# Drawing twelve steps of the next batch's transform into each round, and spacing steps wider from round 4 on

## The chip, the core and the metric

The kernel runs on one core of a Trainium2 chip. The metric is the device time of one execution in microseconds (us). Before the change the median of three runs is 1286.0 us (1285.17 to 1287.41).

## What is computed

A Fourier mixing layer is followed by a mixture of experts in which every token goes to one expert.

```python
X = np.fft.fft(np.fft.fft(x, axis=1), axis=2).real      # x: (8, 2496, 256)
x = X.reshape(19968, 256)
logits = x @ w_gate                                     # 8 experts
e = argmax(logits, axis=1)
gate = softmax(logits)[n, e]
out[n] = gate * (relu(x[n] @ w1[e]) @ w2[e])            # w1: 256x1024, w2: 1024x256
```

## The kernel before

**Transform.** Each of the 8 batches is transformed in two stages. `first(b)` (L327) loads the batch in three pieces `xq` (L291, 0.9 MB each), folds them on DVE (L297 to L299, L308), multiplies them on PE (product `s`, `half1` at L313), copies the product to `t` on ACT (L323) and writes it to DRAM as `Td` (L344, 448 KB each). It has twelve yields, so twelve steps, three for each q from 0 to 3: those of q = 0 only fold, those of q = 3 only multiply. In the third step of q = 1, 2 and 3 it writes a `Td` piece and asks for one piece of the batch after (`load`, L346). `ahead_of(b)` (L888) runs `first(b)` and then `regroup` (L353), which reads `Td` back in another order into `t4` with two DMAs of 768 and 640 KB, in packets of 1 KB.

`second(b)` (L363) works on `t4`: `turn_last` (product `pr`), `group` (product `p<-table,t`, evicted by ACT into `zz`), then ten steps in two halves of five, each with a product `p<-table,zz` that gives a tile of transformed rows and their logits. After each half `route` (L418) finds the expert and the place of each row, in four parts; the third is the PE product `rk`. At its end ten row tiles are put in `waiting`. `send` (L464) takes one from there, converts its places on ACT (L469) and scatters it to `Xs` with an indirect DMA that POOL issues (L237). `close(b)` runs `plan` (L478), which works out on DVE which expert each block of the round has; its tables then stand in `tabs`. `through(b)` waits until all row tiles of the batch have been sent, and then puts the batch in `whole`.

`mixed(b)` (L894) weaves these into the steps of one round: three steps of `ahead_of(b + 1)`; then `second(b)` with 19 yields, after every other one of which a step of `ahead_of(b + 1)` is run; then `close(b)` with the `regroup` of batch b + 1; then `through(b)`.

**Experts.** `experts` (L713) runs blocks of 512, 256 or 128 sorted tokens, one expert to a block. A block fetches its rows `xb` from `Xs` and 2 MB of weights `w_sb`, both on SP's queue and up to three blocks ahead. Its first product is `ph` (or, in blocks of 512 tokens from batch 3 on, seven products with the tiles `a` to `e`), evicted as `hT` by ACT and DVE in turn (L810, L808); its second product is `py` from `hT`, evicted by ACT as `y` (L849) and scattered to the output. `hT` has one buffer. Batch 0 gives two blocks of 256 and four of 128, batch 1 four of 256, batch 2 three of 512, batches 3 to 6 five of 512 each, batch 7 five of 512 and the rest.

**The order around the change.** The whole order is written out by hand: each engine's instructions stand in the order in which this code issues them. The loop at L954 has one turn for each round b from 1 to 7. In it the blocks of batch b - 1 run, with the steps of `mixed(b)` beside them. Each yield of `experts` brings a weight w and says whether it is "full" (no step may follow it) or open. For an open one, `due` grows by

```python
due += TICKS * w / ((SHARE if b >= LATE else EARLY) * open_) if w else 1
```

(L971), and one step is run for each whole 1 in `due`. `open_` is the open weight of the round: 32 in rounds 1 and 2, 48 in round 3, 40 in rounds 4 to 7. `TICKS` is 32, so a round's first 32 steps take 70% of its open weight in rounds 1 to 3 and 60% in rounds 4 to 7. In round 1 the steps of batch 0's `close` and `through`, and what is left of `early` (batch 1), are woven with those of `mixed(1)` (L958). Steps left over when the blocks are done are run in a row (L981).

Of the kernel before, what the change touches and what calls it, by code (L numbers as in the profile page):

```python
# [3 lines left out]

# [1 line left out]

# [14 lines left out]
B, S, D = 8, 2496, 256  # L21
# [110 lines left out]
def rounds():  # L132

    want = [((256, 2), (128, 4)), ((256, 4),)] + [((512, B),)] * (B - 2)
    plan, used = [], 0

    def full(done, size):
        return max(0, -(-(done - used - E * (size - 1)) // size))  # L140

    for b in range(B):
        done = (b + 1) * S
        now = []
        for size, most in want[b]:
            k = min(full(done, size), most)
            if k:
                now.append((size, k, False))
            used += size * k
        if b == B - 1:  # L150
            k = full(done, BLK)
            used += BLK * k
            now.append((BLK, k, False))
            now.append((REST, (NT - used + E * (REST - 1)) // REST, True))
        plan.append(now)
    return plan
# [27 lines left out]

TICKS = 32
LATE = 4
SHARE, EARLY, ROOM = 0.6, 0.7, 1.2
WARM = 16
MOST = max(k for now in rounds() for _, k, _ in now)

# [1 line left out]
def halved(b, size):  # L192

    return size == 512 and b > 2 or size == 256 and b == B - 1
# [22 lines left out]
def kernel(ctx: ExitStack, tc, x, w_gate, w1, w2, out):  # L217
# [49 lines left out]
    side = [n for n in consts if n not in ("w1", "rt")]  # L267
# [196 lines left out]
    def send():  # L464

        if waiting:
            b, place, idx, rows = waiting.popleft()
            if b:
                act.copy(idx, place)  # L469
            sent(put_row(Xs, idx, rows, E * CAP - 1, "xs"), b)  # L470
# [397 lines left out]
    def woven(*parts):  # L868
        parts = list(parts)
        while parts:  # L870
            for p in list(parts):
                if next(p, p) is p:
                    parts.remove(p)
                else:
                    yield

    def close(b):

        for size, k, last in rounds()[b]:
            yield from plan(b, size, k, last)  # L880

    def through(b):

        while waiting and waiting[0][0] == b:
            yield
        whole.add(b)

    def ahead_of(b):  # L888

        yield from first(b)  # L890
        regroup(b, 0)
        regroup(b, 1)

    def mixed(b):  # L894

        one, two = (ahead_of(b + 1) if b + 1 < B else iter(())), second(b)
        for _ in range(3):
            next(one, None)
            yield
        for k, _ in enumerate(two):  # L900
            if k % 2:
                next(one, None)
            yield
        yield from woven(close(b), one)
        yield from through(b)
# [43 lines left out]
    for k, _ in enumerate(second(0)):  # L949
        if k % 2 == 0:  # L950
            next(early, None)
        send()
    work = experts(todo)
    for b in range(1, B):  # L954

        side, done, due, room = mixed(b), 0, 0.0, 0.0
        if b == 1:
            side = woven(chain(close(0), through(0)), chain(early, side))  # L958
        blocks = [(size, k * size / BIG, halved(b - 1, size)) for size, k, _ in rounds()[b - 1]]
        total = sum(k * (15 if seven_ else 16) for _, k, seven_ in blocks)  # L960
        open_ = sum(k * (8 if seven_ else 16) for _, k, seven_ in blocks)
        while done < total:
            w, full = next(work)
            done += w
            if full and not w:

                while waiting:
                    send()
                whole.update(p[0] for p in tabs if p != "cnt")
            if not full:  # L970
                due += TICKS * w / ((SHARE if b >= LATE else EARLY) * open_) if w else 1  # L971
            while due >= 1:
                next(side, None)
                due -= 1
                if b < LATE or not w:
                    send()
            room = min(room + (w if full else 0.75 * w), 2)
            if b >= LATE and room >= ROOM:
                send()
                room -= ROOM  # L980
        for _ in side:  # L981
            send()
# [52 lines left out]
```

## Time and profile before

| view | value |
|---|---|
| profiled execution | 1297.33 us (span 1295.5 us) |
| median of the runs | 1286.0 us |
| mean granted TensorE clock | 0.971 |
| DVE, ACT, POOL busy | 700.5, 423.4, 360.6 us |
| DMA over the span | 249.75 MB, 193 GB/s |
| PE's longest waits by line: `s` on DVE's fold | 10.9 us in 3 |
| `pt` on the rows `xb` | 7.3 us in 2 |
| `ph` on `hT` by DVE | 6.7 us in 3 |

The profiled execution is 11.3 us longer than the median, so a stall in the trace need not be in the timed runs at its full size. Busy time of PE is a union of pipelined matmuls; gaps in it are real waits of the PE queue, which takes its matmuls in order. "Releaser" in the views is the instruction whose semaphore came last by the records. Times in the views are from the span's start.

### The profile page before, as it was taken

To read this page: it belongs to the slowest core of one execution; us is meant where nothing else is said; L and a number is where in the kernel's file an instruction comes from. 1 tells how busy PE (TensorE), PEld (TensorE's weight loads), DVE (VectorE), ACT (ScalarE), POOL (GpSimd) and SP (SyncE) were. 2 spreads that over 40 slices of the span, in tenths; PEclk is the share of its full clock that TensorE was granted. 3 is DMA by queue.
4 is the path that set the end of the run, shared out by engine and by line. 5 is a ranking of instruction groups with operands and counts; after the bars stand their busy time and mean duration, and the time that the engine had idled before them with its cause. 6 is when DMAs were issued, how large, how long until landed. Compare 5 with 4: busy or idle time off the path is not lost.

```text
span 1295.5 us, 20735 instructions
## 1 busy us (share of the span) xinstructions
PE 1237.7 (96%) x7003; PEld 1090.5 (84%) x7003; DVE 700.5 (54%) x1772; ACT 423.4 (33%) x1059; POOL 360.6 (28%) x355
## 2 busy tenths in 40 slices
PE   6769899899999999999999999999999999999997
PEld 4658788687688888888888888888889999999996
DVE  4554145244256655566356655467488774444662
ACT  1423133132244333443234333343333332222222
POOL 0244304314411531135111531145364221111112
PEclk6869999999999999999999999999999999999998
DMA  8877857726636853456433744344355237777776
GB/s 240 275 237 270 310 205 254 276 84 201 201 114 176 277 152 110 141 150 242 120 102 127 241 128 149 98 135 146 107 151 164 90 113 288 276 265 273 290 294 241
DMA packets 134023, 249.75 MB, mean 193 GB/s; under 512 B 85065, under 2 KB 99891, under 8 KB 114332
## 3 DMA queue, kind: packets, MB, share of 16 engines
q1 hardware_dynamic: 117143, 203.33, 48.3%
q0 software_dynamic: 15888, 42.14, 9.0%
q10 hardware_dynamic: 885, 2.94, 0.7%
q8 instruction: 57, 0.93, 0.3%
q14 instruction: 50, 0.41, 0.1%
HBM read 194.97 MB, written 54.83 MB: 193 GB/s over the span
## 4 chain that ended last, share of the span: by engine, by line
PE 70%; issue 18%; DMA 4%; POOL 3%; DVE 2%; another core or an unknown queue 2%; ACT 1%; SPq 0%; POOLq 0%; ACTq 0%; DVEq 0%
PE py L222 28%; PE a L222 7%; PE c L222 7%; PE ph L222 6%; PE p L222 5%; PE d L222 4%; PE b L222 4%; PE s L222 3%; PE e L222 3%; POOL out_dram L237 3%; DMA xq<-in_x_dram 2%; PE pt L595 1%; DMA Xs<-rows,pi 1%; DMA xb<-Xs 0%
## 5 line engine op out<-in xcount | busy, mean ns | idle before, releaser
L222 PE MATMUL py<-w_sb,hT 128*128 128x256 f32 x2016 | 455.9, 381 | 6.5 <-DVE hT L808 3.9
L222 PEld LDWEIGHTS py<-w_sb,hT 128*128 128x128 f32 x2016 | 379.5, 191 | 57.2 <-DVE hT L808 4.3
L237 POOL DMA_INDIRECT out_dram<-y,ro x163 | 160.8, 986 | 729.2 <-ACT y L849 497.9
L237 POOL DMA_INDIRECT Xs<-rows,pi x160 | 163.3, 1020 | 198.3 <-ACT pi L469 103.6
L222 PE MATMUL ph<-xT,w_sb 128*128 128x128 f32 (+2 forms) x992 | 172.4, 329 | 8.5 <-DVE hT L808 6.7
L222 PEld LDWEIGHTS ph<-xT,w_sb 128*128 128x128 f32 x992 | 136.1, 193 | 34.1 <-issue 17.2
L849 ACT ACTIVATE y<-py,xb 128x256 f32<-128x256 f32 x129 | 61.0, 473 | 313.5 <-PE py L222 271.6
L222 PE MATMUL a<-xT,w_sb 128*128 128x256 f32 (+1 forms) x512 | 117.5, 356 | 0.0
L808 DVE TENSOR_SCALAR hT<-ph 128x512 f32<-128x512 f32 x43 | 29.7, 691 | 161.9 <-issue 79.7
L633 DVE TENSOR_TENSOR u<-p,b 128x512 f32<-128x512 f32 x57 | 39.2, 687 | 132.9 <-PE b L222 96.7
L222 PEld LDWEIGHTS a<-xT,w_sb 128*128 128x128 f32 x512 | 89.2, 190 | 10.3 <-issue 0.2
L643 ACT ACTIVATE hT<-a 128x512 f32<-128x512 f32 x57 | 34.0, 597 | 151.2 <-PE a L222 133.6
L410 DVE COPY lg<-p 128x16 f32<-128x16 f32 x80 | 13.9, 174 | 121.0 <-ACT zs L407 117.5
L222 PE MATMUL s<-xq,w 104*112 104x256 f32 (+2 forms) x208 | 62.9, 427 | 11.1 <-DVE xq L299 10.9
L810 ACT ACTIVATE hT<-ph 128x512 f32<-128x512 f32 x55 | 32.8, 597 | 98.2 <-PE ph L222 71.0
L222 PEld LDWEIGHTS p<-table,t 120*128 120x128 f32 x352 | 54.3, 204 | 12.3 <-issue 6.6
L222 PE MATMUL p<-table,t 120*128 120x120 f32 (+1 forms) x352 | 58.2, 290 | 3.8 <-issue 2.7
L222 PE MATMUL c<-xT,ws 128*128 128x256 f32 (+1 forms) x256 | 59.1, 358 | 2.3 <-issue 1.7
L222 PE MATMUL p<-table,zz 128*128 128x145 f32 (+1 forms) x320 | 56.8, 302 | 3.8 <-issue 2.0
L222 PE MATMUL d<-xT,w_sb 128*128 128x256 f32 (+1 forms) x256 | 58.8, 357 | 0.0
L222 PE MATMUL e<-xs,w_sb 128*128 128x256 f32 (+1 forms) x256 | 58.7, 356 | 0.0
L222 PE MATMUL b<-xs,ws 128*128 128x256 f32 (+1 forms) x256 | 58.7, 356 | 0.0
(148 smaller groups left out, 1739.1 us busy)
## 6 DMA issues: line engine op xcount, KB each, us to landing
w_sb<-in_moe_w_dram SPq DMA_DIRECT2D x132, 1024.0 KB
xq<-in_x_dram SPq DMA_DIRECT2D x24, 896.0 KB
xb<-Xs SPq DMA_DIRECT2D x100, 128.0 KB
Td<-t SPq DMA_DIRECT2D x18, 448.0 KB
t<-Td SPq DMA_DIRECT2D x8, 768.0 KB
t<-Td SPq DMA_DIRECT2D x8, 640.0 KB
xb<-Xs SPq DMA_DIRECT2D x25, 129.0 KB
Td<-t ACTq DMA_DIRECT2D x6, 448.0 KB
```

Source lines behind the costliest of these rows:

```text
L222: nc.tensor.matmul(o, lhsT=lhsT, rhs=rhs, start=start, stop=stop, **kw)
L237: return unordered(pool.indirect_dma_start(out=dst, out_offset=bass.IndirectOffsetOnAxis(ap=idx, axis=0), in_=rows, in_offset=None, bounds ...
L410: vec.tensor_copy(lg[:, k:k + 2], p3[:, NY:NY + 2 * E].rearrange("p (m e) -> p m e", m=2))
L595: nc.tensor.transpose(pt[:, c, t], xb[:, 2 * h + t, c:D:2], ident[:])
L633: vec.tensor_tensor(u2[:], p1[:], b[:], op=add)
L643: act.activation(h11, a[:], ACTF.Relu)
L808: vec.tensor_scalar(o, ph[:], 0.0, None, op0=ALU.max)
L810: act.activation(o, ph[:], ACTF.Relu)
L849: act.activation(y[:], py[:], ACTF.Copy, scale=meta[:, i, 1:2])
```

## The change

At the top of the loop's turn b the steps are now `mixed(b)`, followed by the first twelve steps of `mixed(b + 1)`. The generators of all rounds are made ahead of the loop, so that the next turn goes on where this one stopped. In round 1, `TICKS` is 44 in place of 32. `SHARE`, which sets the pace of rounds 4 to 7, goes from 0.6 to 0.8.

```diff
-SHARE, EARLY, ROOM = 0.6, 0.7, 1.2
+SHARE, EARLY, ROOM = 0.8, 0.7, 1.2
+AHEAD = 12
...
     work = experts(todo)
+    steps = {b: mixed(b) for b in range(1, B)}
     for b in range(1, B):

-        side, done, due, room = mixed(b), 0, 0.0, 0.0
+        done, due, room = 0, 0.0, 0.0
+        side = chain(steps[b], islice(steps.get(b + 1, iter(())), AHEAD))
+        ticks = TICKS + AHEAD * (b == 1)
         if b == 1:
             side = woven(chain(close(0), through(0)), chain(early, side))
...
-                due += TICKS * w / ((SHARE if b >= LATE else EARLY) * open_) if w else 1
+                due += ticks * w / ((SHARE if b >= LATE else EARLY) * open_) if w else 1
```

The twelve steps of `mixed(b + 1)` are: three folding steps of `first(b + 2)`, then nine steps of `second(b + 1)` (`turn_last`, two `group` steps, the five steps of its first half, and the first part of `route`), with four more steps of `first(b + 2)` among them.

More of the change, by code (lines that the diff above doesn't have):

```diff
@@ L2 @@
 from contextlib import ExitStack, contextmanager
-from itertools import chain
+from itertools import chain, islice
 import numpy as np
```

## The prediction

> **What bounds the kernel now.** I read the busy shares and the clock row of the page first, then a table of stages, then PE's timeline where a stage shows a hole.
>
> ```profile
> PE 1237.7 (96%) x7003; PEld 1090.5 (84%) x7003; DVE 700.5 (54%) x1772; ACT 423.4 (33%) x1059; POOL 360.6 (28%) x355
> PE   6769899899999999999999999999999999999997
> PEclk6869999999999999999999999999999999999998
> ```
>
> PE is nearly always busy, and its holes are at the start. The table of stages (stage, length, busy us and instructions of PE, weight loads, DVE, ACT and POOL, then granted clock, DMA share, GB/s) says where:
>
> ```profile
> 97.00:130.00 33.00, 30.75 (x181) 27.00 (x178) 16.01 (x70) 10.67 (x41) 15.77 (x17) 1.00 0.80 272
> 130.00:162.00 32.00, 26.77 (x173) 24.42 (x172) 3.25 (x9) 4.03 (x11) 10.47 (x11) 0.95 0.83 309
> 227.00:259.00 32.00, 27.29 (x104) 19.84 (x103) 6.73 (x11) 4.14 (x11) 9.73 (x10) 0.95 0.75 275
> 389.00:453.00 64.00, 64.00 (x339) 56.64 (x338) 41.82 (x126) 26.83 (x73) 22.20 (x22) 1.00 0.73 226
> 518.00:648.00 130.00, 129.81 (x662) 114.79 (x661) 72.93 (x187) 50.05 (x128) 39.15 (x39) 1.00 0.53 163
> ```
>
> From 389 us PE has no holes. The two stages with 5.2 and 4.7 us of idle PE are those in which DVE works only 3.25 and 6.73 us: the transform's steps of rounds 1 and 2 have run out, and expert blocks stand alone. PE's timeline there (start, length, work, and in brackets the idle time before it and its releaser; the last line is from round 4):
>
> ```profile
> 131.01 3.73 PE L222 MATMUL ph<-xT,w_sb 128*128 128x128 f32 x32
> 134.58 0.40 PE L595 MATMUL pt<-table,xb 128*128 128x128 f32 x2
> 136.31 1.99 PE L222 MATMUL py<-w_sb,hT 128*128 128x256 f32 x8 [1.33 <-issue]
> 142.20 3.54 PE L222 MATMUL py<-w_sb,hT 128*128 128x256 f32 x8 [3.90 <-DVE hT L808]
> 145.58 3.73 PE L222 MATMUL ph<-xT,w_sb 128*128 128x128 f32 x32
> ...
> 239.91 2.80 PE L222 MATMUL ph<-xT,w_sb 128*128 128x256 f32 x8 [3.77 <-DVE hT L808]
> ...
> 462.07 13.98 PE L222 MATMUL py<-w_sb,hT 128*128 128x256 f32 x64
> ```
>
> PE ended `ph` at 134.7, and DVE began the eviction that waits for it only at 141.45, after 13.23 us without work, which the trace puts down to "remote". I can't name the cause. What coincides, here and at 239 us, is a DMA share of 0.9 or more, scatters of row tiles at one per 1.28 us on POOL, and the `regroup`: of its 1 KB packets nearly all fall in 130 to 136 us, though it was issued at 121.4.
>
> [...] After both holes the same eight matmuls are slower: 3.54 against 1.99 us. The granted clock explains it. [...] By the idle rows alone hole A (131 to 146 us) costs 1.33 + 3.90 = 5.2; with the half clock (3.54 − 1.89, the 1.89 being such a group's warm length elsewhere) 6.9. Hole B (233 to 248) costs 0.94 + 3.77 = 4.7; with 2.80, 1.06 and 4.12 us in place of 1.89, 0.63 and 3.62 it is 6.6. I take the larger sums. [...]
>
> [...] I take 0 for `SHARE`, not 200.
>
> **The change, part by part.**
>
> *Where steps run.* I walked through the loop's arithmetic. Before, round 1 runs 42 steps and is out of them at open weight 18 of 32 (the first 128-token block); round 2 at 25 of 32; round 3 at 37 of 48; rounds 4 to 6 at 53 of 75 of the full weight. After, round 1 takes 54 steps at 1.96 per unit of weight in place of 1.43 and ends at 20 of 32; rounds 2 and 3 end where they did, since each gives twelve and takes twelve; rounds 4 to 6 end at 57 of 75. Nothing is left to be run in a row. `whole` comes earlier: round 1 at 12 or so in place of 18, round 2 at 17 in place of 25, round 4 at 38 in place of 53. Up to the first expert block (88 us) the order is the same, so the 33 us of holes before it stay.
>
> *What moves.* Per round, on PE: 7 groups × 0.44 + 5 logit products × 0.51 + 2 `half1` × 0.86 + 2 `pr` × 0.14 = 7.6 us. On DVE: two folds × 2.76 and 1.22 of a third, 5 × 0.7 for rows, 1.4 for `route` = 11.7. On ACT about 7. On SP: one `Td` write and one `xq` load, 1.34 MB, at the 400 GB/s of the full DMA stretches 3.4 us. No scatter moves up: the twelve steps stop before the end of `route`. PE's sum is unchanged; round 1 gets 7.6 us more and round 7 about 6 less. In round 7 there is nothing to fill, so this pays only where it lies in a hole.
>
> *Hole A.* The 128-token block has now two product steps and a `half1` between its two `ph` groups (2.8 us), and two more (2.0) between the second and `py`. [...] If the lateness comes from the scatters, these now end about 10 us earlier, and all 6.9 go. I take 5.3.
>
> *Hole B.* It is in the last block of round 2, still without steps, but scatters end two blocks sooner and the fill stands right ahead of it. Lower end 0, upper 6.6; I take the middle, 3.3.
>
> *What it costs.* Bursts of four steps in a row where there were three: such bursts stall 0.28 us at 107 and 0.3 to 0.45 around 45 us, for a want of PSUM or `zz`; about five bursts, 1.5. The scatters and `regroup` of batch 1 are pressed into the 256-token block before, whose present hole is 1.97 us at 120 (`ph` on `hT`): bound 0 to 2, I take 1.
>
> *Waits for data moved up.* `pr` is on PE's queue, so a late `t4` stops everything behind it. `regroup` of batch 2 went out at 121.4 and was used at 172.8, 51 us later. Now 3.5 + 0.6 + 7.5 + 6.9 = 18.5 us of PE work lie between the last `Td` write and `pr`; the `regroup` must first see that write land (about 3 us), and took 15 us when two weight DMAs of 1 MB stood ahead of it on SP. Now it is ahead of them on the queue, so I take it as in time, with little to spare. In round 4 the distance is 26 us and the packets took 13. `xq` has 25 us.
>
> *Sum.* 5.3 + 3.3 − 1.5 − 1 = 6.1 us off the profiled 1297.3. As that execution is 11.3 longer than the median, some of its holes may be of its own making; I count 5 for the timed runs: **1281**.
>
> **Rivals.** (1) *The holes only move.* The lateness follows the scatters and the `regroup` into blocks which have no steps either (the first half of the second 256-token block). For it: the coincidence above. Gain 0: 1286, within 2.6. (2) *More goes.* A, B and the 1.97 all vanish: 6.9 + 6.6 + 2 − 1.5 = 14, so 1272. Against it: the 11.3 us. (3) *`t4` comes too late* (slower). If the packets of batch 2's or 3's `regroup` end more than 15 us after issue, PE stands at `pr` for the rest; at 6 us late in both rounds, with 1.7 us of half clock each, 15 lost less 6 gained: 1295. It decides from about 3 us late in both. For it: 15 us measured in this very round. Against it: the shorter queue ahead. (4) *New holes in rounds 4 to 7*, at 0 today, so that they can only grow; 4 us would be slower, 1288. (5) *Leftover steps in one burst:* excluded by the count above.
>
> **Chances.** Forecast 0.44, holes move 0.17, more goes 0.13, `t4` late 0.18, new holes 0.08. A change of 0.2% (2.6 us) is what these runs can tell from none. Of the forecast 0.38 is faster by that and 0.06 within; rival 1 is within 0.13, slower 0.04; so faster 0.51, same 0.19, slower 0.30. The range is 1271 to 1294; the forecast's own is 1276 to 1284.
>
> **What would show it.** Right: the stages around 130 to 150 and 233 to 250 with under 2 us idle and a clock of 1.00, `p<-table` between `ph` groups of 128 tokens, the middle unchanged at full PE. Wrong: a wait of `pr` on the DMA `t<-Td` over 2 us (rival 3), holes on `hT` some 10 us earlier (rival 1), or idle PE after 390 us (rival 4).

## The result, and the profile after

| | before | after |
|---|---|---|
| median of six runs each | 1286.83 us | 1277.13 us |
| ratio | | 0.9929, 95% interval 0.9913 to 0.9945 |
| profiled execution, span | 1297.33, 1295.5 us | 1280.35, 1278.5 us |

In this comparison the change takes 9.7 us off. Runs on three more chips are told below. There the kernel before takes 1302 to 1307 us; the whole change was run on two of the three, where it gains 0.1 to 0.2% with intervals that reach beyond 1.000. The profiled execution after is one of the six timed ones. The profiled execution before is not: its six took 1285.17 to 1287.85 us.

The table of stages after the change, in the columns used before (stage, length, busy us and instructions of PE, weight loads, DVE, ACT, POOL, then clock, DMA share, GB/s):

```profile
130.00:150.00 20.00, 19.69 (x141) 18.21 (x140) 8.59 (x33) 8.53 (x25) 6.87 (x8) 1.00 0.86 300
227.00:250.00 23.00, 23.00 (x112) 19.09 (x111) 6.74 (x23) 5.42 (x14) 2.92 (x3) 1.00 0.64 213
389.00:518.00 129.00, 129.00 (x653) 114.27 (x652) 75.07 (x174) 49.61 (x118) 32.78 (x33) 1.00 0.51 163
```

The first two of these stretches before the change:

```profile
130.00:150.00 20.00, 14.77 (x93) 13.19 (x92) 1.67 (x4) 2.48 (x8) 8.55 (x9) 0.91 0.79 290
227.00:250.00 23.00, 18.29 (x80) 15.30 (x79) 2.84 (x5) 2.47 (x8) 8.76 (x9) 0.93 0.79 298
```

The two stages that had holes are full, at full clock, and DVE has work in them. PE's timeline shows the first 128-token block with its fill:

```profile
135.00 1.95 PE L223 MATMUL ph<-xT,w_sb 128*128 128x128 f32 x16
136.79 0.60 PE L223 MATMUL p<-table,t 120*128 120x120 f32 x4
...
139.92 1.95 PE L223 MATMUL ph<-xT,w_sb 128*128 128x128 f32 x16
141.70 0.60 PE L223 MATMUL p<-table,t 120*128 120x120 f32 x4
...
144.03 3.62 PE L223 MATMUL py<-w_sb,hT 128*128 128x256 f32 x16
...
213.75 0.37 PE L223 MATMUL pr<-t,table 120*120 120x6 f32 x2 [1.00 <-DMA t<-Td]
```

`p<-table` now stands between the two `ph` groups and between them and `py`, and `py` runs in one piece. The last line is the price of drawing up: in round 2 `pr` waits 1.00 us for the `regroup`. From 95 us to its last matmul PE's idle time falls from 20.9 to 6.7 us, and the two stretches of 3.4 us in which the clock was 0.50 (from 141.96 and from 240.95 us) are gone: it is 1.00 from 95 to 260 us.

The two spans differ by 17.0 us, where the timed runs show 9.7. The two traces are not of one kind. SP's register instructions show it (line, queue, operation and count, then shortest, median and longest in ns, between 95 and 260 us). Before:

```profile
L550 SPq FUSED_REGOPS  x10: 37/37/700, 120.5 to 253.5; - x10
```

After:

```profile
L551 SPq FUSED_REGOPS  x10: 37/37/42, 123.2 to 248.6; - x10
```

The same instruction takes 37 ns, or once 700. Of SP's hundred FUSED_REGOPS, MOVE and SEQ_ASSERT instructions in this stretch, five take over 300 ns in the trace before, and none after. The traces also differ in how many semaphore events (records of one engine telling another that it may go on) they hold: 15,559 after, 12,338 before. The traces of all twelve runs below are of the kind of the trace before: they hold 12,052 to 12,561 events, have slow register instructions, and evictions in them are late. So the difference of these two traces is not the effect of the change alone, and there is no trace of the kernel before of the other kind.

### The profile page after: what moved, and what is told of

Read it like the earlier page. It is cut to its first block, busy times and chain, and to the rows that moved or that the text cites. A ratio compares the mean times of both kernels' runs of the same rounds, so it can differ in the third digit from the quotient of the medians.

```text
span 1278.5 us, 20743 instructions
## 1 busy us (share of the span) xinstructions
PE 1230.2 (96%) x7003; PEld 1089.0 (85%) x7003; DVE 703.2 (55%) x1772; ACT 425.4 (33%) x1059; POOL 364.6 (29%) x355
## 4 chain that ended last, share of the span: by engine, by line
PE 70%; issue 17%; DMA 4%; DVE 3%; POOL 3%; SPq 1%; ACT 0%; POOLq 0%; ACTq 0%; DVEq 0%
PE py L223 29%; PE c L223 7%; PE a L223 7%; PE ph L223 6%; PE p L223 6%; PE d L223 4%; PE b L223 4%; PE e L223 3%; PE s L223 3%; POOL out_dram L238 3%; DMA xq<-in_x_dram 2%; DMA t<-Td 1%; PE pt L596 1%; DVE s L793 0%; DVE xq L309 0%
## 5 line engine op out<-in xcount | busy, mean ns | idle before, releaser
L238 POOL DMA_INDIRECT Xs<-rows,pi x160 | 166.1, 1038 | 192.2 <-ACT pi L470 76.0
L223 PEld LDWEIGHTS s<-xq,w 104*112 104x112 f32 x208 | 38.6, 202 | 24.0 <-DVE xq L300 11.8
```

The lines of the kernel that those rows point to most:

```text
L223: nc.tensor.matmul(o, lhsT=lhsT, rhs=rhs, start=start, stop=stop, **kw)
L238: return unordered(pool.indirect_dma_start(out=dst, out_offset=bass.IndirectOffsetOnAxis(ap=idx, axis=0), in_=rows, in_offset=None, bounds ...
```

## Experiments

Two explanations of the gain stood against each other. *Fill*: the twelve steps fill the holes at the end of rounds 1 and 2. *Spacing*: the wider spacing of rounds 4 to 7 brings it. The first of the three chips is one where the kernel before takes 1307.08 us (24 runs).

**The twelve steps alone** (edited against the change).

```diff
-SHARE, EARLY, ROOM = 0.8, 0.7, 1.2
+SHARE, EARLY, ROOM = 0.6, 0.7, 1.2
```

> The change with SHARE left at 0.6. Fill (the gain is twelve steps laid into the holes at the tail of rounds 1 and 2): 1277, ratio 0.992 to 0.994, as the whole change. Spacing (the gain is the wider spacing of rounds 4 to 7): 1283 or more, ratio 0.997 to 1.000.

Measured: 1317.72 us, ratio 1.0093 (1.0069 to 1.0116). Neither explanation had it: slower than before. New holes of 2.8 to 2.9 us stand in the seven products at 437, 588 and 740 us. The first of them:

```profile
436.92 1.18 PE L223 MATMUL c<-xT,ws 128*128 128x256 f32 x4 [2.79 <-DVE hT L640]
```

**The wider spacing alone** (edited against the kernel before).

```diff
-SHARE, EARLY, ROOM = 0.6, 0.7, 1.2
+SHARE, EARLY, ROOM = 0.8, 0.7, 1.2
```

> Only SHARE from 0.6 to 0.8, no twelve steps. Fill: 1287 within 2, since rounds 4 to 7 have no holes in PE (ratio 0.999 to 1.001). Spacing: 1277 to 1283, ratio 0.992 to 0.997.

Measured: 1312.57 us, ratio 1.0049 (1.0027 to 1.0070). It is slower too, again against both.

**The pace of round 1 alone** (edited against the kernel before).

```diff
-                due += TICKS * w / ((SHARE if b >= LATE else EARLY) * open_) if w else 1
+                due += (TICKS + 12 * (b == 1)) * w / ((SHARE if b >= LATE else EARLY) * open_) if w else 1
```

> Only the pace of round 1 from 32 to 44, so that steps and scatters of round 1 come earlier, no twelve steps. Fill: no gain, the tail of round 1 is emptier than before; 1286 to 1289, ratio 0.999 to 1.002. Pace (the holes came from scatters and the regroup colliding with the last blocks of the round, and the change gains by sending them earlier): half the gain, round 1's part, 1281 to 1283, ratio about 0.996, and in the profile no hole of PE between 125 and 150 us.

Measured: 1307.50 us, ratio 0.9998 (0.9986 to 1.0011), as *fill* had it. PE's timeline has the hole, but 9 to 12 us earlier than in the traces of the kernel before, at the `py` of the second 256-token block:

```profile
125.08 2.75 PE L222 MATMUL py<-w_sb,hT 128*128 128x256 f32 x12
132.98 6.10 PE L222 MATMUL py<-w_sb,hT 128*128 128x256 f32 x20 [5.14 <-issue]
```

Here the round's steps and scatters came sooner, and the hole came sooner, at its full size: 5.14 us, where the first trace of the kernel before has 3.90 and the one on the second chip 5.28.

**The twelve steps in rounds 1 and 2 alone** (edited against the change).

```diff
-        side = chain(steps[b], islice(steps.get(b + 1, iter(())), AHEAD))
+        side = chain(steps[b], islice(steps.get(b + 1, iter(())), AHEAD if b < 3 else 0))
```

(with `SHARE` 0.6)

> Twelve steps drawn up in rounds 1 and 2 alone; SHARE 0.6; rounds 4 to 7 as before, round 3 with twelve steps fewer. Fill: 1277 to 1279, ratio 0.992 to 0.995, except for what round 3's emptier tail costs. A gain in the later rounds (they too profit from drawing up): 1281 or more, ratio over 0.996.

Measured: 1305.06 us, ratio 0.9982 (0.9964 to 1.0000). This is no gain of the size that *fill* named (0.992 to 0.995). Against the first experiment it leaves out the twelve steps from round 3 on, so that one's loss is made in the later rounds.

The gain that *fill* named came in none of these runs, so both kernels were traced again on a second chip.

**The kernel before, once more.** No edit.

> The kernel before, for its profile on the chip of this call: the four runs so far were on a chip where it takes 1307 us in place of 1287. If the holes in PE behind late evictions of hT come with the chip, its profile shows more than 21 us of idle PE after 95 us where it takes over 1300, and under 15 where it takes 1287. Ratio 1.000 within 0.002.

Measured: 1303.55 us, ratio 0.9998 (0.9974 to 1.0022), and PE is idle for 23.1 us after 95 us. That is over the 21 that late evictions would give.

**The whole change, once more.** No edit.

> The whole change, on the chip of this call. Fill (twelve steps in the holes at the tail of rounds 1 and 2): ratio 0.992 to 0.995 on any chip, no hole over 2 us between 95 and 260 us. Holes that only move (they follow the scatters and the 1 KB packets of the regroup): where the chip has late evictions, a hole of 5 us or more at 125 to 135 us and one at about 210, as in the run with twelve steps in rounds 1 and 2 alone, and a ratio of 0.998 or more.

Measured: 1299.10 us, ratio 0.9988 (0.9966 to 1.0010). This and the trace are what holes that only move would give. PE's timeline of the kernel before on this chip:

```profile
137.87 1.99 PE L222 MATMUL py<-w_sb,hT 128*128 128x256 f32 x8
145.15 3.78 PE L222 MATMUL py<-w_sb,hT 128*128 128x256 f32 x8 [5.28 <-DVE hT L808]
```

and of the change:

```profile
125.25 2.75 PE L223 MATMUL py<-w_sb,hT 128*128 128x256 f32 x12
133.03 6.68 PE L223 MATMUL py<-w_sb,hT 128*128 128x256 f32 x20 [5.02 <-DVE hT L809]
139.55 0.28 PE L223 MATMUL pr<-t,table 120*120 120x6 f32 x2
140.34 1.38 PE L223 MATMUL p<-table,t 120*128 120x120 f32 x10 [0.19 <-ACT t L375]
```

The hole of the 128-token block is filled here too, but one of the same size has opened in the block before it, ahead of the first drawn-up product (`pr` at 139.55). DVE's row for the late eviction is of the same kind as that of hole A in the first trace of the kernel before (the first row here):

```profile
141.45 0.69 DVE L808 TENSOR_SCALAR hT<-ph 128x512 f32<-128x512 f32 x1 [13.23 <-remote]
132.29 0.69 DVE L809 TENSOR_SCALAR hT<-ph 128x512 f32<-128x512 f32 x1 [9.14 <-remote]
```

The sums over 95 to 255 us say what is left of the gain. Before, on this chip:

```profile
sum 160.00, PE 145.75 PEld 128.42 DVE 56.94 ACT 39.45 POOL 53.61; mean PE 29.15 PEld 25.68 DVE 11.39 ACT 7.89 POOL 10.72
```

The change, on this chip:

```profile
sum 160.00, PE 146.98 PEld 130.25 DVE 68.05 ACT 45.96 POOL 54.03; mean PE 29.40 PEld 26.05 DVE 13.61 ACT 9.19 POOL 10.81
```

The change, in the trace of the result:

```profile
sum 160.00, PE 157.21 PEld 137.29 DVE 71.56 ACT 48.74 POOL 56.66; mean PE 31.44 PEld 27.46 DVE 14.31 ACT 9.75 POOL 11.33
```

Of 160 us, PE is idle 14.3, 13.0 and 2.8. The last two are the same instructions in the same order. What differs in this stretch is how late evictions are: PE waits 10.0 us for `hT` by DVE in the one (95 to 260 us), and 1.1 in the other.

**The regroup behind the scatters**, in the kernel before.

```diff
-        yield from woven(close(b), one)
-        yield from through(b)
+        yield from close(b)
+        yield from through(b)
+        next(one, None)
+        yield
```

> The kernel before, with the regroup put behind through(b), so that its packets of 1 KB don't run beside the scatters of the round. If late evictions come from the two together: the holes at about 135 and 236 us go or fall under 2 us, ratio 0.991 to 0.996. If from the scatters alone or from the weights' DMAs: holes as in the kernel before, ratio 0.999 to 1.002. If from the regroup alone: holes of the same size, 10 to 20 us later.

Measured: 1302.51 us, ratio 0.9993 (0.9972 to 1.0013). The hole is where it was, though the 1 KB packets of the `regroup` now run from 145.3 to 151.1 us, after it:

```profile
138.54 1.99 PE L222 MATMUL py<-w_sb,hT 128*128 128x256 f32 x8
145.84 3.62 PE L222 MATMUL py<-w_sb,hT 128*128 128x256 f32 x8 [5.30 <-DVE hT L808]
```

So this hole needs no 1 KB packets, alone or with the scatters; scatters and weights are still beside it, and were not taken away.

**Fourteen steps before the first block**, in the change.

```diff
-                for _ in range(9):
+                for _ in range(14):
```

> The change, with 14 in place of 9 steps between the fetch of the first block's rows and its first product, where PE waited 4.5 to 6.9 us for the rows. If those steps fill that wait: 3 to 5 us less than the change in the same call. If the rows come as late after as before, and the tail of round 1 is emptier: the same within 2 us.

Measured: 1300.36 us, ratio 0.9984 (0.9956 to 1.0013), beside 0.9988 for the change: nothing to be told apart. The first `ph` starts at 97.5 in place of 88.8 us. The wait for the rows is filled, but four `p<-table,t` take 1.05 and 1.19 us there (from 86.48 and 92.93 us), where they take 0.60 from 99.30 on. A wait of 2.93 us ahead of `rk` lies in it too, and the five steps take longer than the wait they replace.

On a third chip the question was whether the gain returns. It does not.

**The kernel before, a third time.** No edit.

> The kernel before once more, for its profile where this call runs. Late evictions decide: if it takes 1287, its profile has holes behind hT of under 5 us in all between 95 and 260 us; if it takes 1300 or more, of 9 us or more, as on the two chips so far.

Measured: 1302.50 us, ratio 0.9994 (0.9974 to 1.0014). The holes are 5.27 us from 138.5 on and 0.96, 2.42 and 2.39 at 221 to 242, which is over the 9 us in all that late evictions would give.

**The whole change, a third time.** No edit.

> The whole change. Fill: ratio 0.991 to 0.995 wherever it runs. Late evictions: 0.991 to 0.995 only where it takes under 1285 and its profile has no hole behind hT over 2 us; 0.997 to 1.001 where the kernel before takes 1300 or more, with a hole of about 5 us near 130 us.

Measured: 1300.39 us, ratio 0.9979 (0.9958 to 1.0001), again with a hole at `py` of the second 256-token block:

```profile
136.04 6.57 PE L223 MATMUL py<-w_sb,hT 128*128 128x256 f32 x20 [6.47 <-DVE hT L809]
```

**Rounds 1 and 2 alone**, as on the first chip.

> Twelve steps drawn up in rounds 1 and 2 alone. Fill: the same ratio as the whole change within 0.002. If the later rounds matter: 0.003 or more above the whole change.

Measured: 1301.20 us, ratio 0.9995 (0.9973 to 1.0017). That is within 0.002 of the whole change, and neither can be told from no gain.

**The twelve steps alone**, as on the first chip.

> Twelve steps in every round, SHARE 0.6. If the pace of rounds 4 to 7 only decides where scatters meet the seven products: 1.007 to 1.011 and holes behind u or hT near 434, 585 and 737 us where evictions come late; the same as the whole change within 0.002, and no such holes, where they don't.

Measured: 1315.25 us, ratio 1.0086 (1.0053 to 1.0119): the loss of the first experiment is there again. PE's waits between 400 and 900 us (total, times, longest), with `SHARE` at 0.6:

```profile
PE c L223 <- DVE hT L640: 11.5, 4, 3.0
```

and with 0.8, the whole change on the same chip:

```profile
PE a L223 <- ACT hT L644: 1.7, 4, 0.6
```

With the twelve steps and the old pace, rounds 4 to 7 get a hole of some 2.9 us each, in the seven products, where a product follows its eviction within a few products. With the new pace they get almost none.

## Why the prediction was right, and where it wasn't

**The time.** 1281 was forecast and 1277.13 measured, within the forecast's own 1276 to 1284. Of the rivals that named a size, *more goes* (1272) lies on the other side, 5.1 us off where the forecast is 3.9 off. Part of this is luck. Nothing measured stands behind counting 5 of the 6.1 us for the timed runs, and on two further chips the same change is worth 1.2 and 2.6 us.

**Hole A.** The forecast took 5.3 of 6.9 us. No run shows hole A cut short with the clock at full, so the 5.3 was the author's estimate. In the trace of the result the hole is gone as a whole (0.31 us idle and a clock of 1.00 from 130 to 150 us), and 1.95 us of `ph` is followed by transform products as the step said. **Hole B** was taken at 3.3, the middle of 0 and 6.6; it is gone too, so the upper end was right in that trace. **Bursts** were priced at 1.5 us; the bursts of round 1 in that trace (from 102.59 and from 108.41 us) show no gap over 0.25 us. **The pressed block** was priced at 1 us more; its hole went from 1.97 to 1.07. These four terms make the sum of the forecast, 6.1, too small for that trace, and the measured 9.7 lies between it and the 14 of *more goes*.

**The holes only move** had a chance of 0.17. On the other chips it is what both traces of the whole change show, in the block that it named, the second of 256 tokens, though at `py` and not in the first half. There the change is worth 0.1 to 0.2%. The chance was set for one outcome. Which of the two holds goes with how late evictions are in an execution, and the trace of the kernel before alone did not show that evictions can come in time.

**What coincides.** The prediction named a DMA share of 0.9 or more beside both holes. At 239 us that is a misreading. The share is 1.02 from 230 to 233 us, but PE stands from 236.1 on, DVE's eviction starts at 239.16, and there the row is

```profile
236.00:240.00 4.00, 0.23 (x2) 0.09 (x1) 0.69 (x1) 0.60 (x1) 0.97 (x1) 1.00 0.32 86
```

So this eviction came 3.0 us late at a DMA share of 0.32, and the load of the DMA engines at that moment is not the cause of every hole.

**`SHARE` at 0.** This step failed on the two chips where it was tested. The trace before has 64 `py` matmuls of round 4 in 13.98 us, 216 ns apart, and the author's estimate was that spacing does nothing there; no run shows the 200 us that stood against it. Rounds 4 to 7 had next to nothing to win, but much to lose: the spacing makes the kernel 0.5% slower when it is alone, and about 1% faster when the twelve steps are there (on the third chip 1315.25 without it, 1300.39 with it). Rival 4 had the place, new holes in rounds 4 to 7, and took them for a fault of the whole change. They come when one of its two halves is left out: between 400 and 900 us PE waits 11.5 us in four waits without the spacing (third chip), and 4.3 us in six with the spacing alone (first chip). (PE was not quite full after 389 us before the change either: it is idle for 5.9 us up to its last matmul, but for 0.6 of them only between 389 and 907.) Why one pace meets the late evictions inside the seven products and the other doesn't was not settled. If the packets of the `regroup` were the cause, they would lie inside that phase in the run with holes. On the third chip the phase starts at 575.0 us in both runs, and the packets end ahead of it in the run with holes (572.0) and inside it in the other (577.8).

**`t4` too late.** Rival 3's wait is there, once after 95 us, at 1.00 us, under the 2 us named as its sign. In round 1, where the margin was reckoned smallest, `pr` does not wait. In round 2 the argument against the rival failed: two weight DMAs went out at 197.3 and 197.8 us, ahead of the `regroup` at 198.8, and its packets ended 16 us later, at 214.8.

**The profile against the median.** The 11.3 us between them were read as a sign that some holes may not be in the timed runs. That fits: the three traces of the kernel before are of executions of 1297 to 1303 us, and all have late evictions, while the timed runs it stood beside took 1285 to 1288. That those had fewer late evictions is likely and not shown, since none of them has a trace.

**Clock.** Four of the long gaps come with a low clock after them: 0.53 from 142.20 to 145.58 us after the 3.90 of the first trace of the kernel before, 0.68 from 239.91 to 242.71 after its 3.77, and 0.50 from 145.1 to 151.0 after the 5.28 on the second chip. With the change on that chip the clock is 0.84 from 128 to 150 us, where the gap of 5.02 lies. But the length alone does not decide. In the kernel before on the second chip a gap of 2.00 us at 121.4 is followed by this row (columns as in the table of stages):

```profile
123.40:127.40 4.00, 4.00 (x12) 3.22 (x13) 3.55 (x19) 0.86 (x4) 1.95 (x2) 0.57 1.02 325
```

The clock is 0.57 there, where a gap of 1.97 us in the first trace left it at 1.00 (121 to 128 us). With the change on the same chip a gap of 3.17 us lies in this stretch and leaves the clock at full (1.00 from 200 to 225 us):

```profile
206.00:214.00 8.00, 4.83 (x25) 4.00 (x24) 3.98 (x15) 0.86 (x4) 4.46 (x5) 1.00 0.98 332
```

What stays open: why evictions are late in thirteen of fourteen traces, and whether it is the chip or something else that differs from one comparison to the next; whether recording the trace has a part in it, as the smaller number of semaphore events may suggest; and what share of the 9.7 us is fill, since there is no trace of the kernel before without late evictions.

## What to carry to other kernels

Before two traces are subtracted, check that they are of one kind: the same cheap instruction should take the same time in both (here it took at most 42 ns in one, and once 700 in the other), and the number of recorded events should agree (here 15,559 and 12,338). A fill has to stand ahead of the product that waits: on the second chip the wait came earlier with the change, and a hole of 5.02 us opened in a nearby block that has no fill there. And an engine that is full in a stage is no reason to price a reordering of that stage at zero: here PE was idle for 0.6 us from 389 to 907 us, so that there was next to nothing to gain, and the wider spacing alone cost 5.5 us (1312.57 for 1307.08).

## What the runs showed of the hardware

With the DMA engines full (a share of 1.02 and 404 GB/s from 127 to 136 us, the twelve steps alone, first chip) the consumer of a PE product starts 8.7 us after the product's end by the records (127.17 to 135.85 us), with nothing on its own engine in between:

```profile
125.18 1.99 PE L223 MATMUL ph<-xT,w_sb 128*128 128x256 f32 x8 [1.89 <-DVE hT L809]
135.85 0.69 DVE L809 TENSOR_SCALAR hT<-ph 128x512 f32<-128x512 f32 x1 [10.73 <-remote]
```

In the trace of the result, under the same load (1.04 and 398 GB/s from 200 to 214 us), three evictions follow this run of `ph`, eight matmuls to each, 216 ns apart; the second product ends at about 211.0 us, and DVE starts at 211.12:

```profile
207.40 5.34 PE L223 MATMUL ph<-xT,w_sb 128*128 128x256 f32 x24
211.12 0.69 DVE L809 TENSOR_SCALAR hT<-ph 128x512 f32<-128x512 f32 x1 [7.01 <-PE ph L223]
```

So here full DMA engines alone did not make the evictions late. The same program spans 1278.5 us in one execution and 1303.0 in another (third chip), whose mean granted clocks, 0.973 and 0.982, differ by 0.009, with the longer at the higher clock. Of the difference, 18.7 us are idle PE after 95 us, and about 4 a later first block.
